# RWKV-7 recurrence and hardswish FFN: five slots a unit on two PSUM pairs from unit nine on

## The chip, the cores and the metric

The kernel runs on one core of a Trainium2 chip. The metric is device microseconds of one execution; the kernel before takes 798.61 us as the median of three runs (797.54 to 799.25). The engines are TensorE (PE, with its weight loads as PEld), VectorE (DVE), ScalarE (ACT), GpSimd (POOL) and SyncE (SP), which issues the DMAs. All data are 32-bit floats.

## The reference

The inputs r, k, v, w, a, b have the shape (B, H, S, D) = (4, 8, 768, 40). A recurrence over S runs for each batch and head, and its outputs are the input of a feed-forward network (FFN).

```python
state = zeros(B, H, D, D)
for t in range(S):
    y[:, :, t] = einsum('bhd,bhde->bhe', rt, state)
    Sa = einsum('bhde,bhe->bhd', state, at)
    state = state * wt[:, :, None, :] - einsum('bhd,bhe->bhde', Sa, bt) \
            + einsum('bhd,bhe->bhde', vt, kt)
x = y.transpose(0, 2, 1, 3).reshape(B * S, H * D)      # 3072 x 320
h = x @ w_in                                           # 320 x 2048
out = (h * clip(h + 3, 0, 6) / 6) @ w_out              # 2048 x 320
```

## The kernel before

**Units.** The 768 steps are cut into blocks of 64 steps (BL = 64, two halves of L = 32), and the four batches into two pairs. One unit i is one block of 64 steps of one pair of batches; there are NK = 24, numbered from 0, in groups of NU = 4 (two blocks of steps of both pairs), so unit nine is i = 8. Within a block the recurrence is written as small matrix products of 40 to 64 rows, one for each head, issued so that four of them fill the four quarters of the 128x128 array.

**Stages.** The work of a unit is cut into stages, each a Python generator: it issues its products on PE, yields, and then issues what other engines do with the result. Those of `prepare` do not need the state and are issued units ahead: W turns the decays w and makes their running products (two scans on DVE), gam writes these out, A, B and K turn and scale a, b and k, F is the product of the turned b and a, `factor` turns the factors back (and makes KBt, the scaled k and b side by side), E is the masked product of a and k, EV its product with v. The stages of `step` need the unit before: RT and VT turn r and v; R is the state times a, S the state turned back, C the masked product of r and v, U and UT the solved corrections and their turn, rS the product of r with the state, H the masked product of r and U, sn the state's sums, y the outputs' sums. After y, DVE adds into ys, POOL multiplies ys by gam into yg, and `move` and `move2` bring yg to the FFN's layout xt by four DMAs each on SP's queue. `move2` brings the last 64 of the 320 columns.

The system that U solves is inverted for a group of four units at a time (`invert`): steps of two DVE or POOL instructions, dealt out between the pieces of other work, and a last part with products (`third_blocks`).

**FFN.** The generator `feed_forward` runs jobs, two for each unit: `expand` makes a quarter of PE's work a piece (w_in times xt, four matmuls of 128 columns each), with a part for the last 64 rows of x (`short`), ACT and DVE make hardswish of it (gt), and `contract` multiplies the gt of the job before by w_out into the PSUM bank "o". A job can begin when `ready[i]` holds the xt of its unit.

**Order.** Nothing is scheduled by a tool: every engine runs its instructions as the code issues them. For i = 4 and later a unit has four blocks (`a_block(m)`), with the stages of each block listed in OWN_STAGES and AHEAD_STAGES. In a block, `together` issues first all products in the order of PRODUCTS, as far as five PSUM banks reach, and then the rest in the order of RESULTS:

```python
OWN_STAGES = [["RT", "VT"], ["R", "C", "S"], ["U", "UT", "rS"], ["sn", "H"], ["y"],
              ["move", "move2"]]
AHEAD_STAGES = [["W", "gam"], ["A", "B"], ["F", "K"], ["E", "factor"], ["EV"]]
RESULTS = ["RT", "y", "W", "VT", "EV", "R", "S", "C", "A", "B", "move", "move2",
           "U", "UT", "rS", "F", "K", "sn", "H", "E", "factor", "gam"]
```

A sixth entry of OWN_STAGES falls into the second block of the next unit, so `move` is issued one block after y. Between blocks `feed` issues FFN pieces at a rate of 3.5 (6.2 where steps of an inversion are dealt out).

**PSUM.** There are eight banks: "one" for whole turns, "o" for the FFN's result, two for h, and two pairs of two banks for everything else. W, K and the state are turned whole by `turn_pairs` and in S, four transposes of 128x128 into the bank "one"; r, v, a and b are turned by `turn_halves`, eight transposes of 64 rows into a pair, which puts two heads' 40 values into halves of 64.

**Lines that the prediction names**: L484 half turns, L512 the scores (C, H, E), L520 the mask, L544 and L555 the scans of W, L568 gam's copies, L690 EV, L878 the state's turn, L949 and L957 sn, L972, L983 and L984 y, ys and yg, L998 and L1003 move and move2, L1054 and L1095 the FFN's products, L1070 its hardswish.

Of the kernel before, what the change touches and what calls it, by code (L numbers as in the profile page):

```python
# [31 lines left out]
def kernel(  # L32
# [64 lines left out]
    def bank(tag, shape, bufs):  # L97
        return ps.tile(shape, F32, name=tag, tag=tag, bufs=bufs)

    ring, open_half = deque(), [None]  # L100
    lent = tc.tile_pool(name="lent", bufs=1, space=PSUM)
    pools = {"lent": lent.__enter__(), "pair": ps}
# [14 lines left out]


# [22 lines left out]
    def ps_pair(*dims):  # L141

        n = 1
        for d in dims:
            n *= d
        if shared[0] is None or shared[1] + n > 512:
            shared[:] = pair(), 0
            open_half[0] = None
        at = shared[1]
        shared[1] += n  # L150
        views, step = [], n
        for d in dims:
            step //= d
            views.append([step, d])
        t = shared[0][:]
        return [_ap(t, at, views), _ap(t, at + 512, views), _ap(t, at, [[512, 2]] + views)]

# [53 lines left out]
    wms = [const.tile([P, SCAN + 1], F32, name=f"wm{i}") for i in range(2)]  # L211
# [10 lines left out]
    for i in range(3):  # L222
        t = const.tile([P, H, BL], F32, name=f"score{i}")
        nc.gpsimd.memset(t[:], 0.0)
        score.append(t)
# [208 lines left out]
    def fetch(name, i, engine=None):  # L434

        if i is None or i >= NK:
            return
        x, crossed = {"W": (w, 0), "A": (a, 0), "B": (b, 0), "K": (k, 0), "R": (r, 1),
                      "V": (v, 1)}[name]
        if name == "V":  # L440
            t = values[i % AHEAD]
        else:
            t = placed.get((name, i))
            if (name, i) == ("R", 1):
                t = others["K"]
            t = t if t is not None else (others if i < 2 * NU and i % 2 and name != "R" else inputs)[name]
        g, p = names[i]
        engines = engine or nc.sync
        for q in range(2):
            engine = engines[q] if isinstance(engines, tuple) else engines  # L450
            y = x[2 * p + q, :, g * BL:(g + 1) * BL, :]
            rows = slice(q * BL, (q + 1) * BL)
            if crossed:
                for s in range(2):
                    engine.dma_start(out=t[rows, 4 * s:4 * s + 4, 0:D],
                                     in_=y[s::2].rearrange("h t e -> t h e"))
            else:
                engine.dma_start(out=t[rows, :, 0:D], in_=y.rearrange("h t e -> t h e"))
        data[i][name + "N"] = t
# [38 lines left out]

    def turned(name):
        return tmp.tile([P, NPR, P], F32, name=name, tag="turned", bufs=5)  # L500

# [3 lines left out]
    def scores(lhs, rhs, swap=False):  # L505


        o = ps_pair(NPR, BL)
        for n in range(NPR):
            for q in range(2):  # L510
                for i in range(2):
                    nc.tensor.matmul(out=o[i][half(q), n, :],  # L512
                                     lhsT=lhs[half(i, D), n ^ (2 * q * swap), half(q)],
                                     rhs=rhs[half(i, D), n, half(q)], start=True, stop=True)
        return o

    def masked(o):
        turn[0] += 1
        x = score[turn[0] % len(score)]
        nc.vector.copy_predicated(out=x[:].rearrange("p (i h) t -> p i h t", i=2), mask=mask8, data=o[2])  # L520
        return x


    def prepare(i, F):
        n, o = i % NU, data[i]
        halves = i >= 2 * NU
        def w_stage():
            wt = turn_pairs(o["WN"])
            yield PE

            wm = o["wm"] = wms[i % 2]
            wv = wm[:, 0:SCAN].rearrange("p (r m i) -> p r m i", m=2, i=HB + 1)
            x = wt[:].rearrange("p r (q m i) -> p (r q) m i", q=2, m=2)
            if i == 0:
                nc.vector.tensor_copy(wv[:, :, 0, 1:HB + 1], x[:, :, 0, ::-1])
            else:
                nc.scalar.activation(out=wv[:, :, 0, 1:HB + 1], in_=x[:, :, 0, ::-1], func=AF.Copy)
            if i == 0:
                nc.vector.tensor_copy(wv[:, :, 1, 1:HB + 1], x[:, :, 1, :])
            else:  # L540
                nc.scalar.activation(out=wv[:, :, 1, 1:HB + 1], in_=x[:, :, 1, :], func=AF.Copy)  # L541
            fetch("W", following(i))
            prods = o["prods"] = tmp.tile([P, NB, 2, HB + 1], F32, name="prods", bufs=2)
            nc.vector.tensor_tensor_scan(  # L544
                out=prods[:].rearrange("p r m i -> p (r m i)"), data0=wm[:, 0:SCAN], data1=start[:],
                initial=0.0, op0=ALU.mult, op1=ALU.add,
            )

        def gam_stage():
# [8 lines left out]
            gam = o["G"] = grp.tile([P, NPR, P], F32, name="gam", tag="gam", bufs=NU + 2)  # L558
# [58 lines left out]
        def f_by_64():  # L617

            f = ps_pair(NPR, BL)
# [9 lines left out]
            for z in range(0, P, BL):  # L629
                nc.scalar.activation(out=to[z:z + L, :, :, 0:L], in_=f[2][z:z + L, :, :, 0:L],  # L630
                                     func=AF.Copy, scale=-1.0)
                for c in range(2):
                    nc.scalar.activation(out=to[z + L:z + BL, :, :, c * L:c * L + L],
                                         in_=f[2][z + L:z + BL, :, :, L - c * L:BL - c * L],
                                         func=AF.Copy, scale=-1.0)

        def factor_stage():

            if halves:
                rg = ps_pair(NPR, SLOT)  # L640
                for pr in range(NPR):
                    for s in range(2):
                        nc.tensor.transpose(out=rg[s][:, pr, :], in_=o["rg"][half(s), pr, :],
                                            identity=ident[half(s), half(s)])
# [22 lines left out]
            if i > 2 * NU:  # L667
                fetch("V", i)
# [3 lines left out]
        def k_stage():  # L672
            x = turn_pairs(o["KN"])
            yield PE
            kt = o["kt"] = turned("kt")
            nc.vector.tensor_tensor(out=kt[:], in0=x[:], in1=o["rg"][:], op=ALU.mult)

        def e_stage():
            x = scores(o["kt"], o["at"])
            yield PE  # L680
            o["E"] = masked(x)
# [84 lines left out]
    def third_block(F, tb, tt, n, zs, first=False):  # L766


        parts = [slice(0, H)]
        zp = ps_pair(H, L)  # L770
# [22 lines left out]
        yield DONE  # L793
        tp = ps_pair(H, L)
# [25 lines left out]
    def step(i):  # L820
# [8 lines left out]
        def s_RT():  # L829
            x = turn_in(o["RN"], halves)  # L830
            yield PE
            m["RT"] = turned("RT")
# [40 lines left out]
        def s_S():  # L873

            sp = ps_any([P, 2, 2, P])
# [10 lines left out]
        def s_U():  # L886

            if fresh:
                new_U()
# [11 lines left out]
        def s_C():  # L901
            x = scores(m["VT"], m["RT"])
            yield PE
            m["K"] = masked(x)

        def s_UT():

            up = ps_pair(2, P)
            for j in range(2):
                for s in range(2):  # L910
                    for x in range(2):
                        for rs in range(2):
# [7 lines left out]
            nc.scalar.activation(out=m["UT"][:].rearrange("p (x j) t -> p x j t", x=2), in_=up[2],  # L920
                                 func=AF.Copy, scale=-1.0)
# [37 lines left out]
        def s_H():  # L959
            x = scores(m["UT"], m["RT"], swap=True)  # L960
            yield PE
            m["B"] = masked(x)
# [38 lines left out]
        def s_move2():  # L1001
            for dst, src in m["moves"][4:]:
# [6 lines left out]
                "sn": s_sn, "H": s_H, "y": s_y, "move": s_move, "move2": s_move2}  # L1009
# [38 lines left out]
    def expand(xt, j0, gts):  # L1048
# [9 lines left out]
        def short():  # L1058
# [4 lines left out]
            if begun[0] + begun[1] == 6 * NQ:  # L1063
                results()

        def results():
            for c in range(2):
                gt = ffn.tile([P, NQ, P], F32, name="gt", bufs=5)
# [6 lines left out]
        for c in range(2):  # L1075
            for t in range(2):
# [3 lines left out]
                if c == 1 and t == 1 and not narrow:  # L1080
                    results()
                yield True
# [4 lines left out]
    def contract(i, r, gts):  # L1087
        split = i < SPLIT
        if r == 0 or split:
            op = bank("o", [P, 512], 1)[:, 0:DM]  # L1090
# [29 lines left out]
        yield True  # L1120
# [3 lines left out]
    stream = feed_forward()  # L1124
# [4 lines left out]
    def pieces(n):  # L1129

        owed[0] += n * (8 / 9 if spread[0] else 1)
        while owed[0] >= 1:
            owed[0] -= 1
            if not next(stream):
                owed[0] = 0.0
# [192 lines left out]
    def together(stages):  # L1328
# [3 lines left out]
        def finish():  # L1332
# [5 lines left out]
            shared[0] = open_half[0] = None  # L1338
# [56 lines left out]
    m = 0  # L1395
    for i in range(NU, NK):
        spread[0] = i >= 2 * NU - 1
        for j in range(BLOCKS):
            rate, inversion = 3.5, 0
            if i + AHEAD >= NK + NU - 1:  # L1400
                rate = 4.5
            if i < 2 * NU - 1:
                rate = 2.8
            parts = a_block(m)
            next(parts)
            if side or i % NU == NU - 1 and rate < 4:

                rate, inversion = 6.2, 2 + (i < 2 * NU)
            feed(rate / 2, inversion)
            for _ in parts:  # L1410
                pass
            if i % NU < 2 and j < 2:
                if i % NU == 0:
                    aside(3 * L)
                block(i, j)
            if side:
                rate, inversion = 6.2, 2 + (i < 2 * NU)
            feed(rate / 2, inversion)
            m += 1
    for _ in range(2):  # L1420
        for _ in a_block(m):
            pass
        m += 1
# [33 lines left out]
```

## Time and profile before

| what | value |
|---|---|
| median of three runs | 798.61 us (797.54 to 799.25) |
| profiled execution, span | 802.0 us |
| its last instruction | ACT copy at 798.18 us, then the last output DMAs |
| PE busy | 733.3 us, 91% of the span |
| DVE, ACT, POOL busy | 495.5, 321.2, 175.6 us |
| unit 8 begins (its RT turn) | 317.6 us |
| last y (unit 23) | 758.8 us |
| FFN products, PE busy (L1054, L1095) | 250.4 and 231.8 us |

The profiled execution's own time is its span, 802.0 us; the lines of the profile come from this one execution. In the slices a digit is the busy share in tenths of one fortieth of the span, 20 us; PEclk is the granted clock in tenths. In the windows by engine a row has the stretch, its length, the busy time of each engine with the number of instructions, the granted clock, the DMA engines' share and GB/s. In a timeline a row has the start, the duration, the engine, the line, what is written from what, the number of instructions merged into the row, and in brackets the idle time before it with what ended it.

### The profile page before, as it was taken

What the parts mean: (1) busy time and instruction counts of PE and PEld (TensorE: products, weight loads), DVE (VectorE), ACT (ScalarE), POOL (GpSimd) and SP (SyncE); (2) the same over time, 40 slices, a digit from 0 to 9 for tenths busy, and PEclk for the clock granted to TensorE, in tenths of its full rate; (3) what the DMA queues carried; (4) which work ended last, traced back from release to release, by engine and by line L of the source; (5) the groups of instructions that cost most, each with busy time, mean ns of one, the idle gap of its engine ahead of it and who ended that gap; (6) DMA issues with size and microseconds to landing.
All of it is one profiled execution on the core that took longest, in us unless ns stands there. A gap on an engine that the chain in (4) does not pass through costs nothing.

```text
span 802.0 us, 35325 instructions
## 1 busy us (share of the span) xinstructions
PE 733.3 (91%) x15832; PEld 622.8 (78%) x15832; DVE 495.5 (62%) x967; ACT 321.2 (40%) x668; POOL 175.6 (22%) x318
## 2 busy tenths in 40 slices
PE   5726777999999989999999999999999999999998
PEld 4625665878778868888888888888888888888886
DVE  7896777679555699455698445897444973322210
ACT  2348882321644424543344453324443324422111
POOL 6403012420322222223123123304122202000000
PEclk9855798999999999999999999999999999999999
DMA  9683553420233331233222233213222101110000
GB/s 120 118 198 85 152 142 57 76 46 9 45 57 66 59 56 28 53 64 56 41 45 43 44 58 62 46 34 57 44 51 48 20 20 29 30 25 13 15 19 17
DMA packets 174215, 45.03 MB, mean 56 GB/s; under 512 B 157424, under 2 KB 172784, under 8 KB 174064
## 3 DMA queue, kind: packets, MB, share of 16 engines
q1 hardware_dynamic: 169760, 42.03, 27.7%
q8 instruction: 125, 2.05, 1.1%
q10 hardware_dynamic: 4304, 0.74, 0.7%
q14 instruction: 26, 0.21, 0.1%
HBM read 34.08 MB, written 3.93 MB: 47 GB/s over the span
## 4 chain that ended last, share of the span: by engine, by line
PE 77%; DVE 8%; issue 5%; DMA 4%; SPq 2%; ACT 2%; POOL 1%; DVEq 0%; ACTq 0%; POOLq 0%
PE h L1054 26%; PE o L1095 24%; PE pair L512 4%; PE pair L972 3%; PE pair L484 2%; PE pair L949 2%; PE one L474 2%; PE pair L894 2%; PE pair L856 2%; PE pair L914 1%; PE pair L690 1%; PE pair L930 1%; DMA R<-in_r_dram 1%; DVE wm L555 1%; PE pair L799 1%
## 5 line engine op out<-in xcount | busy, mean ns | idle before, releaser
L1054 PE MATMUL h<-xt,win 128*128 128x128 f32 (+1 forms) x2304 | 250.4, 282 | 3.5 <-DVE gt L1070 3.5
L1054 PEld LDWEIGHTS h<-xt,win 128*128 128x128 f32 (+1 forms) x2304 | 230.8, 192 | 20.5 <-issue 4.2
L1095 PE MATMUL o<-wout,gt 128*128 128x320 f32 x768 | 231.8, 445 | 0.0
L1095 PEld LDWEIGHTS o<-wout,gt 128*128 128x128 f32 x768 | 139.2, 191 | 51.0 <-issue 1.2
L1070 DVE SCALAR_TENSOR_TENSOR gt<-gt,h 128x512 f32<-128x512 f32 x96 | 62.0, 681 | 71.7 <-ACT gt L1069 71.6
L1069 ACT ACTIVATE gt<-h,three 128x512 f32<-128x512 f32 x96 | 62.2, 686 | 100.9 <-PE h L1054 100.5
L984 POOL TENSOR_TENSOR yg<-ys,gam 128x512 f32<-128x512 f32 x22 | 39.0, 1772 | 165.4 <-DVE ys L983 91.2
L741 DVE TENSOR_TENSOR prod<-x 128x30 f32<-128x30 f32 (+9 forms) x180 | 67.2, 373 | 8.8 <-POOL x L726 3.3
L663 POOL TENSOR_TENSOR KBt<-K,rgt 128x320 f32<-128x320 f32 x22 | 19.0, 865 | 215.4 <-ACT rgt L652 166.9
L747 DVE TENSOR_TENSOR x<-x,prod 128x30 f32<-128x30 f32 (+9 forms) x180 | 62.3, 346 | 5.5
L957 DVE TENSOR_TENSOR state<-pair,state 40x320 f32<-40x320 f32 (+1 forms) x44 | 21.4, 487 | 65.9 <-PE pair L949 39.8
L520 DVE COPY_PREDICATED score<-mask,pair 128x512 f32<-128x512 int32 x71 | 49.9, 723 | 1.8 <-PE pair L512 1.4
L983 DVE TENSOR_TENSOR ys<-pair,ys 128x512 f32<-128x512 f32 x22 | 15.2, 691 | 44.7 <-PE pair L690 22.0
L555 DVE TENSOR_TENSOR_SCAN wm<-wm,start 128x528 f32<-128x528 f32 x24 | 37.6, 1565 | 0.8
L544 DVE TENSOR_TENSOR_SCAN prods<-wm,start 128x528 f32<-128x528 f32 x24 | 30.3, 1270 | 10.2 <-ACT wm L541 10.1
L834 ACT ACTIVATE RT<-pair 128x512 f32<-128x512 f32 x21 | 12.5, 597 | 52.9 <-PE pair L484 52.9
L972 PE MATMUL pair<-score,KBt 64*64 64x64 f32 x1472 | 29.2, 232 | 4.0 <-DVE state L957 3.2
L695 ACT ACTIVATE EV<-pair 64x320 f32<-64x320 f32 x44 | 19.0, 432 | 33.5 <-PE pair L690 22.8
L972 PEld LDWEIGHTS pair<-score,KBt 64*64 64x64 f32 x1472 | 25.8, 145 | 6.6 <-DVE state L957 3.7
L809 ACT ACTIVATE tinv<-pair 32x256 f32<-32x256 f32 x48 | 18.0, 375 | 30.1 <-PE pair L799 29.5
L1113 ACT ACTIVATE ob<-o 128x320 f32<-128x320 f32 x22 | 9.6, 435 | 49.1 <-PE o L1095 29.3
L572 POOL COPY gam<-prods 128x256 f32<-128x256 f32 x24 | 22.5, 937 | 29.3 <-DVE prods L544 25.4
(262 smaller groups left out, 1062.6 us busy)
## 6 DMA issues: line engine op xcount, KB each, us to landing
V<-in_v_dram SPq DMA_DIRECT2D x96, 40.0 KB
out_dram<-ob SPq DMA_DIRECT2D x47, 80.0 KB
R<-in_r_dram SPq DMA_DIRECT2D x92, 40.0 KB
B<-in_b_dram SPq DMA_DIRECT2D x42, 80.0 KB
K<-in_k_dram SPq DMA_DIRECT2D x42, 80.0 KB
W<-in_w_dram SPq DMA_DIRECT2D x37, 80.0 KB
A<-in_a_dram SPq DMA_DIRECT2D x37, 80.0 KB
xt<-yg SPq DMA_DIRECT2D x72, 40.0 KB
```

What stands on the lines that cost most here:

```text
L512: nc.tensor.matmul(out=o[i][half(q), n, :], lhsT=lhs[half(i, D), n ^ (2 * q * swap), half(q)], rhs=rhs[half(i, D), n, half(q)], start=True ...
L520: nc.vector.copy_predicated(out=x[:].rearrange("p (i h) t -> p i h t", i=2), mask=mask8, data=o[2])
L544: nc.vector.tensor_tensor_scan(out=prods[:].rearrange("p r m i -> p (r m i)"), data0=wm[:, 0:SCAN], data1=start[:], initial=0.0, op0=ALU.m ...
L555: nc.vector.tensor_tensor_scan(out=back, data0=back, data1=start[:], initial=0.0, op0=ALU.mult, op1=ALU.add)
L741: nc.vector.tensor_tensor(out=pv, in0=_ap(x[:], (i + 1) * L + i, [[L, n], [0, i]]), in1=_ap(x[:], i * L, [[0, n], [1, i]]), op=ALU.mult,)
L747: nc.vector.tensor_tensor(out=rest, in0=rest, in1=pv, op=ALU.add)
L972: nc.tensor.matmul(out=y[q][half(s), pr, :], lhsT=o[name][half(q), h * D:h * D + SLOT], rhs=m[name][half(q), 4 * rs + 2 * s + j, :], start ...
L984: nc.gpsimd.tensor_tensor(out=yg[:], in0=m["ys"][:].rearrange("p r q t -> p r (q t)"), in1=o["G"][:], op=ALU.mult)
L1054: nc.tensor.matmul(out=hp[c][:, i, :], lhsT=lhsT, rhs=rhs, start=(begun[c] == 0), stop=(begun[c] == 3 * NQ - 1))
L1069: nc.scalar.activation(out=gt[:], in_=hp[c][:], func=AF.Relu, bias=three[:], scale=1.0)
L1070: nc.vector.scalar_tensor_tensor(out=gt[:], in0=gt[:], scalar=6.0, in1=hp[c][:], op0=ALU.min, op1=ALU.mult)
L1095: nc.tensor.matmul(out=op[:], lhsT=gts[c][:, n, :], rhs=wout[:, c * HJ + r * NQ + n, :], start=((split or r == 0) and c == 0 and n == 0), ...
```

## The change

From unit nine (i = 8) on, the units run in five slots instead of four blocks; for i = 4 to 7 the old loop stays as `earlier_blocks`.

- `slot(i, j)` issues the products of the stages that SLOTS lists (an offset k with a stage names unit i + k; −1 is the unit before), then the rest in the order of AFTER. FILLS says which stages share a PSUM pair, and there are two pairs only. `gap` issues 2.7 FFN pieces after each slot, 3.5 while an inversion is being dealt out.
- K and W (from i = 13) and the state (from i = 8) are turned by halves, eight transposes into a pair. factor turns 40 values instead of 64.
- `ysn` replaces sn, y and their additions by one product: 32 products with 104 moving columns (64 of the scores and 40 of V or U, side by side in `beside["K"]` and `beside["B"]`) instead of 64 products with 64 or 40. For this POOL copies V, and ACT writes U, into these areas.
- `ysn`, `move` and `move2` stand in one slot.
- F takes four ACT copies instead of six. U, UT and S share pairs. `contract` takes the banks "one" and "o" in turn. There are four gt buffers instead of five, and a buffer's hardswish follows each half (`results(c)`).
- V of unit i + 4 is fetched in C, behind POOL's copy of V.

```diff
     def scores(lhs, rhs, swap=False, placed=False):
-        o = ps_pair(NPR, BL)
+        o = every_other(1) if placed else ps_pair(NPR, BL)
...
         def w_stage():
-            wt = turn_pairs(o["WN"])
+            wt = turn_halves(o["WN"])[2] if late else turn_pairs(o["WN"])
...
         def k_stage():
-            x = turn_pairs(o["KN"])
+            x = turn_in(o["KN"], late)
...
         def s_S():
+            if i >= 2 * NU:
+                sp = ps_pair(4, D)
+                for n in range(4):
+                    for x in range(2):
+                        nc.tensor.transpose(
+                            out=sp[x][:, n, :], identity=ident[half(x, D), half(x, D)],
+                            in_=st[half(x, D), n // 2, 2 * (n % 2):2 * (n % 2) + 2, :].rearrange("p r d -> p (r d)"))
...
         def s_C():
             x = scores(m["VT"], m["RT"])
             yield PE
-            m["K"] = masked(x)
+            if i < 2 * NU:
+                m["K"] = masked(x)
+                return
+            masked(x, beside["K"][:, :, 0:BL])
+            nc.gpsimd.tensor_copy(beside["K"][:, :, BL:JOIN].rearrange("p (r x) d -> p r x d", r=2),
+                                  VN[:].rearrange("p (x r) d -> p r x d", r=2)[:, :, :, 0:D])
+            if i > 2 * NU:
+                fetch("V", i + NU)
...
+        def s_ysn():
+            o2 = ps_pair(NPR, JOIN)
+            for name in "KB":
+                for pr in range(NPR):
+                    j, rs = pr // 2, pr % 2
+                    for s in range(2):
+                        for q in range(2):
+                            h = 2 * pr + s
+                            nc.tensor.matmul(
+                                out=o2[q][half(s), pr, :], lhsT=o[name][half(q), h * D:h * D + SLOT],
+                                rhs=beside[name][half(q), 4 * rs + 2 * (s ^ (q * (name == "B"))) + j, :],
+                                start=(name == "K" and pr == 0), stop=(name == "B" and pr == NPR - 1))
+            yield PE
+            yg = m["yg"] = tmp.tile([P, NPR, P], F32, name="yg", tag="yg", bufs=2)
+            x = m["ys"][:].rearrange("p r q t -> p q r t")
+            nc.vector.tensor_tensor(out=x, in0=o2[2][:, :, :, 0:BL], in1=x, op=ALU.add)
+            nc.gpsimd.tensor_tensor(out=yg[:], in0=m["ys"][:].rearrange("p r q t -> p r (q t)"),
+                                    in1=o["G"][:], op=ALU.mult)
+            for rows in [half(s, D) for s in range(2)]:
+                x = st[rows, :, :, 0:D]
+                nc.vector.tensor_tensor(out=x, in0=o2[2][rows][:, :, :, BL:JOIN], in1=x, op=ALU.add)
...
+    SLOTS = [
+        [(4, "K factor"), (0, "RT VT")],
+        [(5, "A B"), (0, "S R"), (3, "EV")],
+        [(-1, "H"), (5, "F"), (4, "E")],
+        [(6, "W"), (-1, "ysn"), (0, "C"), (-1, "move move2"), (6, "gam")],
+        [(0, "U UT rS")],
+    ]
+    FIRST_SLOTS = {
+        (0, 0): [(0, "RT VT"), (5, "W"), (-1, "y move move2"), (5, "gam")],
+        (0, 1): [(0, "S R"), (4, "EV")],
+        (0, 2): [(5, "A B")],
+        (0, 3): [(6, "W"), (5, "F"), (0, "C"), (6, "gam")],
+        (1, 1): [(5, "A B"), (0, "S R")],
+    }
+    FILLS = ["RT VT".split(), "K factor".split(), "S R EV".split(), "A B".split(),
+             "H F".split(), ["E"], ["ysn"], "W C".split(), "U UT".split(), ["rS"], ["y"]]
+    AFTER = "RT VT factor K S EV A B R H F E y ysn move move2 W gam C U UT rS".split()
+    NORMAL, DENSE, STEPS_OF = 2.7, 3.5, 2.0
...
+    for i in range(2 * NU, NK + 1):
+        for j in range(5):
+            if i == NK and j > 3:
+                break
...
+            slot(i, j)
...
+            gap(bool(side), (lambda: run(blocks[i])) if i < NK and i % NU < 2 and j in (2, 3) else None)
```

## The prediction

> **What bounds the kernel now.** I read the page's busy times and slices first, then the windows by engine over the stretch that is changed, then the timelines of single blocks for the price of each step.
>
> ```profile
> PE 733.3 (91%) x15832; PEld 622.8 (78%) x15832; DVE 495.5 (62%) x967; ACT 321.2 (40%) x668; POOL 175.6 (22%) x318
> PE   5726777999999989999999999999999999999998
> PEclk9855798999999999999999999999999999999999
> ```
>
> PE is short of full in the first third only. The changed stretch begins with unit 8's RT turn at 317.6 us and ends with the kernel at 798.2 us. Two of its windows (span, then PE, PEld, DVE, ACT, POOL, clock, DMA share, GB/s):
>
> ```profile
> 480.00:540.00 60.00, 59.79 (x1221) 51.78 (x1218) 46.25 (x99) 20.40 (x45) 14.67 (x25) 1.00 0.26 48
> 720.00:780.00 60.00, 60.00 (x957) 51.07 (x956) 12.89 (x21) 11.82 (x21) 2.73 (x3) 1.00 0.07 17
> ```
>
> Summed over 300 to 780 us PE is busy 476.7 of 480.0 us, and DVE never above 77% of a window. So here the time is the sum of PE's instructions: PE work taken out is time taken out, and a wait on PE is time added, since 3.3 us is all the idle time there was. The profiled execution spans 802.0 us, 3.4 us over the median 798.61 of three runs; sums are made on the span, and scaled by 0.996.
>
> **PE work that goes.** Prices are from one instruction group's start to the next one's start, in one unit:
>
> ```profile
> 440.36 0.60 PE L878 MATMUL one<-ident,state 128*128 128x128 f32 x4
> 440.89 0.46 PE L484 MATMUL pair<-ident,A 64*128 64x64 f32 x8
> 441.19 0.41 PE L484 MATMUL pair<-ident,B 64*128 64x64 f32 x8
> ...
> 454.76 0.52 PE L949 MATMUL pair<-V,KBt 64*40 64x40 f32 x32
> 455.10 0.55 PE L949 MATMUL pair<-U,KBt 64*40 64x40 f32 x32
> 455.48 0.69 PE L512 MATMUL pair<-RT,UT 40*64 40x64 f32 x32
> ...
> 460.89 1.16 PE L972 MATMUL pair<-score,KBt 64*64 64x64 f32 x64
> 461.88 0.63 PE L690 MATMUL pair<-V,score 64*64 64x40 f32 x32
> ```
>
> A whole turn (state) takes 440.89 − 440.36 = 0.53 us, a half turn (A, B) 0.30 and 0.34, elsewhere down to 0.24: 0.27 taken. W and K change in the 11 units from i = 13, state in 16: 22 × 0.26 + 16 × 0.28 = 10.2 us (state's half turn has 40 rows and columns, so a little less). By 0.34 it is 7.2. Factor 40 wide instead of 64: 11 × 0.04 = 0.4.
>
> State's sums (sn) cost 0.34 + 0.38 = 0.72 us and y 0.99, together 1.71, in 64 records each. In groups of four (the four quarters of the array) that is 45 ns a group for sn and 62 for y. Their product in one has y's 64 records, with 104 columns moving. No row shows 64 weight columns with 104 moving. Lower bound: y's own 0.99, if loading weights sets the pace. Upper: 1.71, nothing saved. The row of the second FFN product gives a rate for moving columns (four records of 320 columns take 1.10 us), 0.276 us / 320 × 104 = 0.090, with 0.007 of start 0.097 a group: 16 × 0.097 = 1.55 us. I take this, since 104 columns are past the 64 at which weights still set the pace: 16 × 0.16 = 2.6 us saved (0 to 11.5). Sum of PE work: −13.2 us, from −7 to −23. Of the old idle time 2 of 3.3 us go too, its blocks being gone: −2 (0 to −3.3). F's fewer ACT copies, U written by ACT, V copied by POOL and four gt buffers lie under FFN pieces on engines at most 77% busy: nothing; without that cover each would be one copy, 0.4 to 0.7 us a unit.
>
> **Wait 1: xt.** Before, yg goes to xt a block after y, and PE never waited for it. Now ysn, the POOL product and all eight DMAs stand in one slot, and the FFN, which has no pieces left over early on, wants that xt in the very next gap. What the chain costs is seen at its last unit, alone:
>
> ```profile
> 758.84 1.16 PE L972 MATMUL pair<-score,KBt 64*64 64x64 f32 x64
> 760.13 0.69 DVE L983 TENSOR_TENSOR ys<-pair,ys 128x512 f32<-128x512 f32 x1 [4.66 <-PE pair L972]
> 760.96 1.27 POOL L984 TENSOR_TENSOR yg<-ys,gam 128x512 f32<-128x512 f32 x1 [22.76 <-DVE ys L983]
> 762.26 3.05 SPq L998 DMA_DIRECT2D xt<-yg  x4
> 765.35 2.46 SPq L1003 DMA_DIRECT2D xt<-yg  x4
> ```
>
> y ends at 760.0. The DMA share of the half-microsecond windows falls to 0.05 at 765.5 (move's four landed by 766.0) and 0.03 at 768.0 (move2's four by 768.2): 6.0 and 8.2 us after y's end. Under load POOL's product takes 2.15 us (518.14), not 1.27, so 7.0 and 9.1. In the built order PE has 3.65 us of instructions between ysn and the first h piece of that xt in unit 9, 2.95 in unit 11, 2.5 in unit 12; move's data are then 3.35, 4.05 and 4.5 us late. One h piece later (0.85 us) the 64-row part wants move2's, 1.25 more each. Sum 4.6 + 5.3 + 5.8 = 15.7 us; with POOL unloaded 12.8, with another POOL copy ahead of it 18. In the other units 6.7 us or more of PE work lie between: nothing, and the pieces that then come late are those of one unit before.
>
> **Wait 2: C's mask.** AFTER puts C's mask on DVE behind W's scans and copies of the same slot; rS stands in the next slot, and as there are two pairs only, its pair is the one that C's mask frees. DVE's queue in that place today:
>
> ```profile
> 488.67 0.69 DVE L983 TENSOR_TENSOR ys<-pair,ys 128x512 f32<-128x512 f32 x1 [3.73 <-PE pair L690]
> 489.28 1.25 DVE L544 TENSOR_TENSOR_SCAN prods<-wm,start 128x528 f32<-128x528 f32 x1
> 490.85 1.87 DVE L555 TENSOR_TENSOR_SCAN wm<-wm,start 128x528 f32<-128x528 f32 x1
> 493.39 1.27 DVE L1070 SCALAR_TENSOR_TENSOR gt<-gt,h 128x512 f32<-128x512 f32 x2
> ```
>
> After ysn ends: ys 0.6, two state sums 1.0, scans and copies 4.1 (489.28 to 493.39), mask 0.7: 6.5 us. PE reaches rS sooner by 3 us in unit 8, 2 in 10, and 0.6, 2.4, 1.3, 1.75, 1.05 in 13 to 17: 12.1 us. In 9, 11 and 12 it hides behind the wait for xt; from 18 on there is no W left. Bounds: 6, if gam's copies go under the gap's pieces, and 16, with one gt product (0.64) ahead of the mask each time. Behind the mask, POOL's copy of V and the next V's fetch in SP's queue are moved too: V lands some 14.8 us after ysn and EV wants it at 15 to 19: nothing, at most 5.
>
> **The clock.** PE without pauses keeps it at 1.00. Where PE paused it often fell:
>
> ```profile
> 172.00:175.00 3.00, 1.41 (x65) 1.21 (x59) 2.86 (x5) 0.18 (x1) 3.00 (x5) 1.00 0.05 8
> 175.00:178.00 3.00, 3.00 (x39) 2.04 (x38) 2.85 (x9) 1.25 (x4) 0.01 (x1) 0.60 0.64 106
> 178.00:181.00 3.00, 3.00 (x25) 3.00 (x24) 2.73 (x8) 0.30 (x1) 0.00 (x0) 0.83 0.23 55
> ```
>
> The loss here is 3 × (0.40 + 0.17) = 1.7 us, after one idle time of 1.59 us. Pauses of 2.9 us at 108 and 3.2 at 129 us were followed by 0.50 in a 3 us window too, at 131 to 137 us two such in a row (about 3 us lost); one of 3.7 at 119 us by none. For the three pauses for xt I take two falls at 2 us: +4 (0 to 9). The Trainium skill ("TensorE: Matmul & The Clock Gate", Part 1: The HAM clock gate) says that a window of about 3.4 us with PE idle throttles it to half, and that it takes a busy window as long to come back. By that rule only the three longest pauses would do it, for 3 × 1.7 = 5.1 us instead of 4; the 1.59 us at 172 speaks for a less strict rule.
>
> **Sum.** −13.2 − 2 + 15.7 + 12.1 + 4 = +16.6 us on a span of 802.0; on the median 798.6 + 16.5, about 815 us. With every term at its end it is −8 to +41; ends do not come together, and 805 to 825 is the forecast's own range.
>
> **Rivals.**
> *The joint product is cheap and the waits short* (faster). One mechanism: the 104 columns ride under weight loads, 0.99 us, saving 11.5 instead of 2.6; for it, U with 40 moving columns takes 0.49 us (447.45 to 447.94) and UT with 64 takes 0.50, so there the columns are free. Against it, 104 columns at FFN's rate already need 0.090 us a group. With the waits at their low ends, without clock falls: −10.6 − 11.5 − 2 + 12.8 + 6 = −5.3, some 793 us. It decides below about 1.0 us for ysn. 0.13.
> *The waits are hidden*: the FFN has pieces of an older unit to run where I read that it has none, or the copies of W go after the mask. Then −13.2 − 2 = −15, 783 us. Against it stands the built order, in which the h pieces right behind these slots name the fresh xt. 0.06.
> *The clock falls after every pause* (slower still): ten pauses of about a microsecond or more, the 1.59 us one being enough before, at 1.7 to 3 us: +17 to +30 instead of +4; about 828 to 840 us. Against it: the 3.7 us pause without one. 0.15.
> *Work and waits cancel*: both at the ends that bring them within 0.2% (1.6 us, about what a measurement of this kernel can tell from no change): 0.03.
> The forecast keeps 0.63. Slower is 0.63 + 0.15 = 0.78, same 0.03, faster 0.13 + 0.06 = 0.19. The range takes the cheap product's 793 and the near end of the clock's case at 830, leaving out the hidden waits and the worst of the clock.
>
> **What would show it.** In the new profile the first h pieces (L1186) of units 9, 11 and 12 should stand behind idle times of 3 to 5 us ended by a DMA of xt, the 64-row part behind 1 us more; rS (L1038) in units 8, 10 and 14 behind 2 to 3 us ended by DVE's mask (L565); ysn (L1082) should take 1.55 us from start to start, half turns 0.27; PE's clock should fall below 0.7 after one or two of the pauses. PE without idle time from 320 us on would make the forecast wrong as a whole, ysn near 1.0 us its saving, and a clock line of many 5 to 8 digits its range.

## The result and the profile after

The changed kernel takes 891.44 us (median of 4 runs, 888.18 to 897.66) against 798.68 us for the kernel before: 1.1179 times as long, 95% interval 1.1136 to 1.1223. The forecast of "slower" was right; its size, 815 us with 830 as the upper end, was far too small.

The page of the changed kernel's profiled execution (span 886.5 us), its busy times, PE's slices and the granted clock:

```profile
PE 770.4 (87%) x14960; PEld 645.5 (73%) x14960; DVE 494.5 (56%) x967; ACT 320.8 (36%) x646; POOL 173.5 (20%) x322
PE   5537779999999988888988798988988999999998
PEclk9855889999999998879998897998989999999999
```

Where PE was at nine tenths from slice 16 on, but for the last, it now has eights and a seven up to slice 31, and the clock has dents in most of the same slices. PE executes fewer instructions and is busy for longer. What it waited for from 317 us on (waits of PE: instruction, releaser, us in total, times, longest):

```profile
PE pair L499 <- DMA B<-in_b_dram: 27.4, 20, 3.8
PE h L1186 <- DMA xt<-yg: 11.0, 4, 4.0
PE pair L1038 <- DVE x L818: 4.7, 2, 3.3
PE pair L1038 <- DVE area L565: 3.1, 4, 1.4
```

The second to fourth rows are the two waits of the prediction. The first and largest is not in it. How it comes about, in the unit i = 10 (units are called by i from here on; timeline of all engines, only the rows of this chain):

```profile
385.40 0.44 ACT L722 ACTIVATE rgt<-pair 128x320 f32<-128x320 f32 x1
386.67 0.46 PE L499 MATMUL pair<-ident,A 64*128 64x64 f32 x8
386.74 0.86 POOL L733 TENSOR_TENSOR KBt<-B,rgt 128x320 f32<-128x320 f32 x1
387.63 1.28 SPq L473 DMA_DIRECT2D B<-in_b_dram  x2
390.22 0.36 PE L499 MATMUL pair<-ident,B 64*128 64x64 f32 x1 [3.09 <-DMA B<-in_b_dram]
```

`factor` ends with POOL's product of B, which is B's last use, and only then can the next unit's B be loaded into the one tile that there is. In the slots, "K factor" stands in the first and "A B" of the unit after in the second, with one gap of FFN pieces between them (2.4 us here). POOL's product ends at 387.60, the load is issued at 387.63 and has landed at 390.2; PE stood there at 387.1. In the kernel before, two blocks lay between: a B issued at 431.02 was turned at 441.19, without a wait:

```profile
431.02 1.27 SPq L458 DMA_DIRECT2D B<-in_b_dram  x2
441.19 0.41 PE L484 MATMUL pair<-ident,B 64*128 64x64 f32 x8
```

The granted clock around this pause (windows: length, then PE, PEld, DVE, ACT, POOL, clock, DMA share, GB/s):

```profile
384.00:387.00 3.00, 3.00 (x30) 2.01 (x24) 1.82 (x4) 1.42 (x3) 1.08 (x2) 1.00 0.23 35
387.00:390.00 3.00, 0.13 (x6) 0.00 (x0) 0.00 (x0) 0.00 (x0) 0.60 (x1) 0.95 0.34 57
390.00:393.00 3.00, 2.43 (x56) 2.17 (x60) 0.00 (x0) 0.00 (x0) 0.00 (x0) 0.50 0.63 109
393.00:396.00 3.00, 3.00 (x40) 2.24 (x33) 1.78 (x3) 1.18 (x3) 0.00 (x0) 0.50 0.14 27
```

From just ahead of unit 8's RT turn (317.0 and 313.7 us) to PE's last product the kernel before has 481.1 us, the changed one 568.9. Adding up PE's starts, and weighing each stretch by its granted clock, that difference of 87.8 us splits into PE idle, 52.0 us instead of 3.3 (+48.7), clock lost while PE worked, 38.0 instead of 0 (+38.0), and PE's work at full clock, 478.9 instead of 477.8 (+1.1). The stretch starts 3.3 us earlier, so the span grows by 84.5. The four rows of waits above make 46.2 of the 52.0 us; 2.3 more are a single wait in unit 8, of the last y in the old form for ACT's copy of VT, which the prediction does not have either.

### The profile page after: what moved, and what is told of

Same layout as the page of the kernel before. It is cut to its first block, busy times and chain, and to the rows that moved or that the text cites. A ratio compares the mean times of both kernels' runs of the same rounds, so it can differ in the third digit from the quotient of the medians.

```text
span 886.5 us, 33539 instructions
## 1 busy us (share of the span) xinstructions
PE 770.4 (87%) x14960; PEld 645.5 (73%) x14960; DVE 494.5 (56%) x967; ACT 320.8 (36%) x646; POOL 173.5 (20%) x322
## 4 chain that ended last, share of the span: by engine, by line
PE 53%; DVE 16%; issue 12%; DMA 7%; SPq 5%; ACT 4%; POOL 3%; POOLq 0%; ACTq 0%; DVEq 0%
PE h L1186 19%; PE o L1227 10%; PE one L1227 5%; DMA B<-in_b_dram 3%; SPq L473 3%; PE pair L539 2%; DVE prods L604 2%; DVE prod L812 2%; PE pair L499 2%; PE pair L1082 2%; DVE x L818 2%; DVE area L615 2%; DMA raw<-in_moe_w_out_dram 2%; PE pair L929 2%; DVE area L565 2%
## 5 line engine op out<-in xcount | busy, mean ns | idle before, releaser
L1186 PE MATMUL h<-xt,win 128*128 128x128 f32 (+1 forms) x2304 | 269.0, 294 | 13.6 <-DMA xt<-yg 11.0
L1227 PE MATMUL o<-wout,gt 128*128 128x320 f32 x480 | 150.1, 454 | 0.0
L1227 PEld LDWEIGHTS o<-wout,gt 128*128 128x128 f32 x480 | 87.9, 195 | 32.1 <-issue 2.2
L1227 PE MATMUL one<-wout,gt 128*128 128x320 f32 x288 | 91.6, 466 | 0.0
L1227 PEld LDWEIGHTS one<-wout,gt 128*128 128x128 f32 x288 | 55.9, 204 | 21.7 <-issue 4.3
L565 DVE COPY_PREDICATED area<-mask,pair 128x512 f32<-128x512 int32 x60 | 44.3, 744 | 24.3 <-PE pair L687 19.8
L1090 POOL TENSOR_TENSOR yg<-ys,gam 128x512 f32<-128x512 f32 x14 | 17.8, 1273 | 175.8 <-DVE ys L1089 129.7
L604 DVE TENSOR_TENSOR_SCAN prods<-area,start 128x528 f32<-128x528 f32 x24 | 32.8, 1374 | 18.3 <-ACT area L595 10.3
L499 PE MATMUL pair<-ident,B 64*128 64x64 f32 x128 | 10.9, 256 | 27.4 <-DMA B<-in_b_dram 27.4
L615 DVE TENSOR_TENSOR_SCAN area<-area,start 128x528 f32<-128x528 f32 x24 | 32.2, 1341 | 0.8
L1082 PE MATMUL pair<-area,KBt 64*64 64x104 f32 x1024 | 26.6, 251 | 0.5 <-issue 0.4
```

The costliest lines, as they stand in the source:

```text
L499: nc.tensor.transpose(out=o[q][:, n, :], in_=x[half(q), 2 * n:2 * n + 2, :].rearrange("p s e -> p (s e)"), identity=ident[half(q), half(q)])
L604: nc.vector.tensor_tensor_scan(out=prods[:].rearrange("p r m i -> p (r m i)"), data0=wm[:, 0:SCAN], data1=start[:], initial=0.0, op0=ALU.m ...
L615: nc.vector.tensor_tensor_scan(out=back, data0=back, data1=start[:], initial=0.0, op0=ALU.mult, op1=ALU.add)
L1082: nc.tensor.matmul(out=o2[q][half(s), pr, :], lhsT=o[name][half(q), h * D:h * D + SLOT], rhs=beside[name][half(q), 4 * rs + 2 * (s ^ (q * ...
L1186: nc.tensor.matmul(out=hp[c][:, i, :], lhsT=lhsT, rhs=rhs, start=(begun[c] == 0), stop=(begun[c] == 3 * NQ - 1))
L1227: nc.tensor.matmul(out=op[:], lhsT=gts[c][:, n, :], rhs=wout[:, c * HJ + r * NQ + n, :], start=((split or r == 0) and c == 0 and n == 0), ...
```

## The experiments

**B with a second place.** The first theory was that late B and the clock falls behind it are most of the loss.

```diff
+            if name == "B" and i > 3 * NU + 2 and i % 2:
+                t = values[NU]
...
-                fetch(name, following(i))
+                fetch(name, i + 2 if name == "B" and i > 3 * NU + 1 else following(i))
...
+            if i == 2 * NU + 1:          # in C, behind the copy of V
+                fetch("B", 3 * NU + 3)
```

> B of odd units from 15 on gets a place of its own (a V tile that is free by then), so each B from unit 15 on is fetched a whole unit before its turn; all else as in the changed kernel. Theory (late B): the changed kernel's time is mostly PE waiting for B, 27.4 us, of which 25.6 belong to these units, and the clock falls right behind eight of these pauses, some 24 us by the windows: about 840 us, mean clock of the stretch from 317 us on up from 0.93 to 0.97. Rival (the waits only change places): the instruction that waited for B then waits for xt or the mask, since the chain of a unit is what lasts: 865 to 885 us, with waits on xt and C's mask grown by over 10 us.

Measured: 845.41 us, 1.0565 times before (1.0526 to 1.0605). Waits of PE:

```profile
PE h L1190 <- DMA xt<-yg: 11.3, 5, 4.1
PE pair L501 <- DMA B<-in_b_dram: 1.8, 2, 1.4
```

B's wait goes but for the one in unit 9, which the edit leaves, and the others stay as they were (xt 11.3 us for 11.0): the rival falls. Idle time falls by 23.0 us and the lost clock by 18.1, so half of the 92 us was this one load. The theory's time, about 840 us, is missed by 5.

**C's mask ahead of W.** The prediction's second wait.

```diff
-    AFTER = "... y ysn move move2 W gam C U UT rS".split()
+    AFTER = "... y ysn move move2 C W gam U UT rS".split()
```

> C's mask stands ahead of W's scans and copies in the order of the other engines, all else as in the changed kernel. Theory of the prediction (second wait): the waits of rS for the mask (3.1 us named, and up to 4.7 more that are put down to an inversion step in front of it) go, with one or two clock falls of 1.7 to 3.4 us behind them: 6 to 12 us less, about 880 us. Rival (the mask's wait is small because W's scans were done by then, and the inversion's steps are what holds it): within 3 us of the changed kernel.

Measured: 885.65 us, 1.1088 (1.1038 to 1.1138), some 6 us less by the medians. The mask's 3.1 us and the 4.7 us are gone, down to 0.6, so both belonged to DVE's order. But B's wait grew from 27.4 to 30.7 us and xt's from 11.0 to 14.4: PE only came sooner to the next one, and idle time fell by less than 1 us. In the profiled executions the stretch from unit 8's RT turn to the last product's start is no shorter (568.5 us, and 568.1 in the changed kernel), so where the 6 us of the medians come from is open.

**Fewer FFN pieces a gap.** The prediction's first wait.

```diff
-    NORMAL, DENSE, STEPS_OF = 2.7, 3.5, 2.0
+    NORMAL, DENSE, STEPS_OF = 2.3, 3.0, 2.0
```

> 2.3 FFN pieces a gap instead of 2.7, and 3.0 instead of 3.5 in the gaps with inversion steps, so that the FFN keeps a store of pieces of an older unit; all else as in the changed kernel. Theory of the prediction (first wait): the 11.0 us of PE waiting for xt go, with four clock falls behind them (some 10 us): minus 20 us. Against that, the gap between B's fetch and its turn is shorter by half a piece, 0.5 us in each of 11 units: plus 6 and perhaps one fall more. Together about 875 us. Rival (no store builds up, the pieces per unit are what the FFN has anyway): 885 to 900 us with the xt waits as before.

Measured: 911.75 us, 1.1397 (1.1349 to 1.1446). Neither expectation holds. The wait for xt disappeared from PE's list, as the theory has it, but the largest row became

```profile
PE pair L499 <- DMA B<-in_b_dram: 44.5, 20, 5.9
```

17 us more, where 6 were expected: the pieces of the gap are the only cover that B's load has. The waits for C's mask grew from 7.8 to 11.1 us too, and those of the inversion's products from 0.5 to 6.5, so more was lost than the 11 us of xt that were gained.

**All three.**

> The three edits together (B's second place, C's mask ahead of W, fewer pieces a gap). Theory: with the waits gone PE is above 98 per cent busy from 320 us on and its clock 1.00, and what is left is the PE work that the change saves, 13 us: about 785 us, below the kernel before. Rival (the change saves no PE work, because the shorter products are set by something other than what the prediction counted): 798 us or more with PE as busy. A second rival: the shared pairs leave PE waiting between a unit's slots even so, with a clock below 0.97: over 810 us.

Measured: 836.49 us, 1.0457 (1.0407 to 1.0507): the second rival's case by its time. PE still waits 28.0 us (the longest group 8.7 us, where the inversion's product waits for E's mask on DVE), 11.8 us of clock are lost, and PE's work at full clock is 477.5 us, the same as before. So the products save nothing in this order, as the first rival has it; why, is taken up below.

**B and C's mask, at the changed kernel's rate.**

> The changed kernel with B's second place and C's mask ahead of W, at the changed kernel's own rate of FFN pieces. Theory (B and the mask are separate waits, each with its falls): below the kernel with B's second place alone by the mask's 8 us and the fall behind the 3.3 us one (3 us): 834 to 838 us, with xt waiting 11 to 14 us. Rival (without the mask's wait PE only reaches the wait for xt sooner): 842 to 846 us with more than 16 us on xt.

Measured: 838.31 us, 1.0457 (1.0422 to 1.0493), just above what the theory gave, with 14.2 us on xt. With B out of the way the mask's edit shortens the profiled stretch from unit 8's RT turn by 5.8 us (518.7 for 524.5), where ahead of B's wait it shortened it by nothing. The smaller rate of the run before, 1.0457 as well, added nothing to it: it took xt's wait away and brought others. Against the kernel before this stretch is still 38.6 us longer: 21.8 us of idle time, 17.8 of lost clock, and 0.9 less of PE's work.

**Pauses in the kernel before.** These runs ask what a pause costs by itself. In the second block of each unit from i = 8 on:

```diff
+    def pause():
+        t = bank("one", [P, 512], 1)
+        nc.tensor.matmul(out=t[:, 0:L // 2], lhsT=ident[:], rhs=pz[:], start=True, stop=True)
+        for _ in range(10):              # 30 in the long one
+            nc.gpsimd.memset(pz[:], 0.0)
+        nc.tensor.matmul(out=t[:, L // 2:L], lhsT=ident[:], rhs=pz[:], start=True, stop=True)
```

> The kernel before with one pause for PE in each of the units 8 to 23, and nothing else changed: a small product reads a tile, POOL then writes that tile ten times, and the next small product on PE waits for that. Estimated pause 1 to 1.3 us, so 16 pauses are 16 to 21 us of waiting. Theory (pauses pull the clock down, and short ones only sometimes): some 4 falls of 1.7 us, 820 to 827 us. Rival (any pause of about 1 us does it): 16 falls of 1.7 to 3.4 us, 845 us or more, clock as low as in the changed kernel.

Measured: 853.28 us, 1.0687 (1.0615 to 1.0759). The pauses were 1.74 us each, longer than estimated: 27.8 us of waiting. Six of the 16 were followed by a fall, which cost 18.6 us of clock, and PE's work from unit 8's RT turn on grew by 9.9 us, as the added products themselves take 11.1 us. The time lies in the rival's range, but the number of falls, 6, is near the theory's 4 and not the rival's 16.

> As the short pause, but POOL writes thirty times: estimated pauses of 2.3 to 3 us, 16 of them 37 to 48 us of waiting. Theory (the changed kernel's falls come from its pauses of 2 to 4 us and from nothing else in it): most of the 16 are followed by a fall, 27 to 45 us of lost clock besides the waiting, 865 to 890 us, although the program is that of before. Rival (the clock falls only after more than 3.4 us without PE work, or only in the changed program): waiting alone, 835 to 848 us, clock 1.00 throughout.

Measured: 947.38 us, 1.1847 (1.1824 to 1.187). The pauses were 5.11 us each, so 81.8 us of waiting, and all 16 were followed by a fall: 61 us of lost clock in a program whose products are those of before. One of them in windows (columns as above):

```profile
398.00:401.00 3.00, 0.00 (x0) 0.00 (x0) 0.00 (x0) 0.00 (x0) 1.97 (x18) 1.00 0.11 25
401.00:404.00 3.00, 2.02 (x22) 1.58 (x22) 0.26 (x1) 0.00 (x0) 0.58 (x6) 0.65 0.24 55
404.00:407.00 3.00, 3.00 (x121) 3.00 (x120) 0.43 (x1) 0.93 (x2) 0.00 (x0) 0.50 0.03 5
407.00:410.00 3.00, 3.00 (x26) 2.88 (x22) 0.22 (x1) 2.49 (x7) 0.00 (x0) 0.50 0.00 0
410.00:413.00 3.00, 3.00 (x19) 3.00 (x19) 2.32 (x3) 0.44 (x2) 0.90 (x4) 0.65 0.02 5
```

The pause is over at 401.9 us, and PE works at half speed for 10 us more although it is full. The time is beyond the theory's 890 us, as the pauses were twice as long as estimated. Both parts of the rival fall: a pause of 1.74 us can be enough, and the program need not be the changed one.

Which of the short pauses bring a fall is not mere chance. In the traces every change of the granted clock lies on a grid of 3.413 us, which a pause meets at any place. The six short pauses with a fall lay within one span of that grid to 1.72 us or more, over half of it. Of the ten without, nine were cut in two by the grid, with at most 1.53 us in one span, and one had 1.72. The pause from 386.48 us (first two rows) and the one from 558.07 (last two), in spans of the grid:

```profile
385.42:388.83 3.41, 1.61 (x9) 1.18 (x8) 0.62 (x2) 0.44 (x1) 1.11 (x10) 1.00 0.15 45
388.83:392.25 3.42, 3.42 (x104) 3.09 (x107) 0.69 (x1) 0.51 (x2) 0.00 (x0) 0.50 0.29 64
556.09:559.50 3.41, 1.98 (x9) 1.33 (x7) 3.31 (x8) 0.42 (x1) 0.91 (x9) 1.00 0.12 31
559.50:562.92 3.42, 3.05 (x135) 2.72 (x135) 3.18 (x9) 0.73 (x2) 0.26 (x3) 1.00 0.04 10
```

Counted over all twelve traces from 200 us on: of 72 such spans at full clock in which PE idled for 1.7 us or more, 70 were followed by a fall; of 1893 with less than 0.9 us, none; of the 139 between, 19.

**The cheaper products in the old blocks.** The stages of the change, with the order of before:

```diff
+    LATE_OWN = [["RT", "VT"], ["R", "C", "S"], ["U", "UT", "rS"], ["H"], ["ysn"],
+                ["move", "move2"]]
...
-            own[i, m] = step(i), OWN_STAGES
+            own[i, m] = step(i), LATE_OWN if i >= 2 * NU else OWN_STAGES
```

> The cheaper products without the new order: W, K, state as half turns, factor 40 wide, y and state's sums as one product, U and UT in one pair and V copied by POOL as in the changed kernel, but issued in the four blocks of the kernel before (ysn where y stood, moves a block later, five V tiles, the old F, 'one' no longer used for whole turns from unit 8). Theory (the products save PE work, and the order is what costs): attention's PE work falls by 9 us as in the changed kernel and PE does not pause, so 790 to 793 us. Rival (the half turns give it back: after an FFN piece a group of 64 rows starts 0.1 us later than a whole turn does, in about 50 of 97 bursts, and blocks must be cut more often to fit two pairs): 797 to 806 us.

Measured: 844.79 us, 1.0551 (1.0519 to 1.0584), outside both. From unit 8's RT turn on (312.8 us here) PE's work at full clock is 3.5 us less than before: attention's groups take 5.6 us less and the FFN's pieces 2.1 more. But PE now waits 44.4 us:

```profile
PE pair L1078 <- ACT area L583: 16.1, 10, 2.4
PE pair L538 <- DVE at L650: 14.8, 11, 1.7
PE pair L1034 <- ACT UT L1024: 11.7, 11, 1.1
```

Each of these is the third pair of a block: ysn behind W's and RT's, C behind the pair of A and B, rS behind U's, as K holds the other. In the kernel before W, state and K went to the bank "one", since a whole turn fills one bank and a half turn takes the same columns of two. So a half turn saves 0.12 (K) to 0.24 us (state) of PE here, and the pair that it takes costs 1.1 to 1.6 us of waiting. Of these 32 pauses, mostly of 1.0 to 1.7 us, only two were followed by a fall (3.4 us of clock); two of 2.4 us, which the grid cuts in two, were not.

**The joint product alone.** As the last one, with W, K, state and factor turned as before.

> As the kernel with the old blocks and the cheaper products, but W, K, state and the factors are turned as before; what is left of the change is y and state's sums as one product (with U and V written beside the masked scores). Theory: 16 x (1.71 + 0.1 at its end - 1.48) = 4 to 5 us less PE work and nothing else: 794 to 796 us. Rival (the joint product comes a block later for the state and pulls a wait behind it, or its 104 columns are dearer in this place): 799 us or more.

Measured: 799.91 us against 799.51, 1.0007 (0.9992 to 1.0022): the rival. The waits name the reason:

```profile
PE pair L757 <- ACT VT L936: 3.6, 11, 0.9
```

ysn is 416 columns wide where y was 256, so EV no longer fits beside it and becomes the third pair of its block.

**EV three blocks later.**

```diff
+    LATE_AHEAD = [["W", "gam"], ["A", "B"], ["F", "K"], ["E", "factor"], [], [], [], ["EV"]]
...
-            ahead[u, m] = prepared(u), CLOSE_STAGES if close else AHEAD_STAGES
+            ahead[u, m] = prepared(u), LATE_AHEAD if u >= 2 * NU + AHEAD else CLOSE_STAGES if close else AHEAD_STAGES
```

> The kernel with the old blocks, whole turns and the joint product, but EV of the units from 13 on is issued three blocks later, where a pair has room for it (beside H), instead of in the block of RT, VT and ysn, where it is the third pair and PE waits for ACT's copy of VT, 3.6 us in 11 units. Theory (the joint product saves its 2 to 4 us of PE work and its width gives them back as that wait): 796 to 797 us, faster than the kernel before by 0.3 to 0.5 per cent. Rival (the saving is smaller than the timelines say, or EV late brings a wait of its own on V's fetch): 799 to 801 us.

Measured: 795.99 us against 800.05, 0.994 (0.9925 to 0.9956): a small gain, 0.6%, but clear of the noise, and at the theory's 796. The wait is gone; from unit 8's RT turn on PE idles 1.4 us (3.3 before) and its work is 3.0 us less than before, where the theory of the joint product alone had 4 to 5. The longest of its waits are

```profile
PE pair L683 <- issue: 0.8, 1, 0.8
PE pair L868 <- DVE area L645: 0.6, 2, 0.3
```

This is what of the change is worth having: y and state's sums as one product, in the old order, with EV where a pair has room.

## Why the prediction was wrong, by its steps

**The step that failed first: the loads that move with a stage.** The prediction followed xt, W and V through SP's queue, and named "the next V's fetch" as the one that is moved past others. `factor` was priced as a turn that is 40 wide instead of 64; that its last lines fetch B and K, and that the next B's turn now stands one slot behind instead of two blocks, was not looked at, so B's wait stood in the sum at nothing. It was 27.4 us. The run without it shows 23.0 us less idle time and 18.1 us less clock loss.

**The clock: mechanism right, size off.** Forecast +4 us, with two falls of 2 us for the pauses for xt; measured 38.0. Falls were looked for behind the three pauses for xt only, and there were thirty pauses of 0.4 to 4 us. The trace has 14 falls: eight behind a wait for B, three behind xt, one behind C's mask, and two behind waits that the prediction does not name. A fall costs more, too: a loss is about 1.7, 3.4 or 5.1 us, 2.7 in the mean here and 3.1 in the run with six, not 2. The rival "the clock falls after every pause" was given 0.15 and 828 to 840 us; even that had the pauses for B missing. By the rule of the Trainium skill that the prediction weighed ("TensorE: Matmul & The Clock Gate", Part 1), only pauses of about 3.4 us do this; here 6 of 16 pauses of 1.74 us did. The unit of the loss agrees with that page of the Trainium skill: one window of 3.4 us at half speed is 1.7 us.

**Wait 1, xt.** Forecast 15.7 us in units 9, 11 and 12; measured 11.0, of which 2.74, 3.91 and 4.02 us were those three. The second of them in PE's timeline:

```profile
451.05 4.15 PE L1186 MATMUL h<-xt,win 128*128 128x128 f32 x24 [3.91 <-DMA xt<-yg]
```

The place and the chain were right. The further 1.25 us for the 64-row part did not come (0.3 us in all), and POOL's product took 1.28 us, as unloaded, not 2.15.

**Wait 2, C's mask.** Forecast 12.1 us, measured 7.8 (3.1 and 4.7, both shown to be the mask's place by the run that moved it). In the run without B's wait it was the same 7.8, so B did not cover for it. Unit by unit, unit 8 is what the sum had wrong, 0.2 for 3 us; unit 10 has 3.3 for 2, units 14 to 17 have 1.4, 1.4, 0.95 and 0.5 for 2.4, 1.3, 1.75 and 1.05.

**PE's work: the size did not come.** Forecast −13.2 us; measured +1.1. ysn was right (1.55 us forecast, 1.48 here, 442.66 to 444.14):

```profile
442.66 1.66 PE L1082 MATMUL pair<-area,KBt 64*64 64x104 f32 x64
444.14 0.65 PE L539 MATMUL pair<-rt,VT 40*64 40x64 f32 x32
```

State's half turn took 0.34 us instead of 0.25, K's 0.27 as forecast, W's 0.39, often as the first group behind FFN pieces. All of attention's groups fell from 149.2 to 141.4 us, −7.8. The FFN's pieces, the same number of instructions, rose from 328.6 to 337.5 us at full clock, +8.9. The prediction's sum has no term for the changes between the FFN and attention, about 90 each way. By the timelines a group of 64 rows or fewer starts 0.08 to 0.09 us later behind a 128-row FFN product than the next FFN product does, and a whole turn no later. Before, 37 of these bursts ran into a whole turn, now none, and the delay behind a burst rose from 0.05 to 0.09 us in the mean: some 4 of the 8.9 us. No run isolates it, and the rest is open. In the old blocks with the same half turns the delay is 0.08 us as well, but the FFN rose by 2.1 us only; so the rest seems to go with the slots' order and not with the half turns as such.

**The rivals.** *The joint product is cheap* is refuted by its 1.48 us. *The waits are hidden* is refuted by the list of waits. The direction was no luck: without B's wait the kernel is still at 845 us, above all by the waits that were named, though that too is beyond 830. The sum of the forecast's kind, with all waits and the clock as measured, is −3.3 (old idle time) + 52.0 + 38.0 + 1.1 − 3.3 (earlier start) = 84.5 us.

## What to carry to other kernels

When a stage is moved, write down every buffer that it is the last to read, and when that buffer's next load is wanted: one tile with one gap between its last use and the next one's turn is a wait in every round, and no engine's busy share shows it. Where PE is full, a pause costs its own length and, when it takes half of a span of the clock's grid, one to three spans of half speed behind it, so ten pauses of 2 us are not 20 us. A product that needs less of PE but a second PSUM bank can lose more on the bank than it gains.

## What the runs showed of the hardware

The granted clock fell after 6 of 16 pauses of 1.74 us and after all 16 of 5.11 us, but after only two of 32 pauses of mostly 1.0 to 1.7 us. It changed only on a grid of 3.41 us, and a fall went with PE's idle time within one span of that grid: 70 of 72 spans with 1.7 us or more of it were followed by one, none of 1893 with less than 0.9. Once it had fallen it stayed at 0.50 for one to three spans, though PE was full again at once; what decides between one and three is open.

A group of PE products of 64 rows or fewer started 0.08 to 0.09 us late behind a 128-row FFN product, a whole turn of 128 rows not at all.
